# The halves of the mixed tensor packed: 344 columns apart in place of 384

## The chip, the cores and the metric

The kernel runs on one core of a Trainium2 chip. A core has a matrix engine (TensorE, PE in the profile, with its weight loads listed apart as PEld), a vector engine (DVE), a scalar engine (ACT), GpSimd (POOL), and queues that start DMA transfers (SP's and ACT's here). They run their own instruction streams and meet through semaphores. The metric is the device time of one execution in microseconds; the time of a kernel is the median of its runs.

## The reference

A layer-normalised input of 2048 tokens by 512 features goes through two branches, which are multiplied and added to the input. Branch A is attention over 32 heads with the last 512 keys of a cache. Branch B is a gated MLP that mixes tokens.

```python
def _B_ref(x, w_in, w_sp, b_sp, w_out):
    z = _gelu(jnp.einsum("bsd,df->bsf", x, w_in))
    z1 = z[..., :Fh]                                   # Fh = 688
    z2 = _layernorm(z[..., Fh:], axis=-1)
    g = jnp.einsum("ts,bsf->btf", w_sp, z2) + b_sp[None, :, None]
    return jnp.einsum("bsf,fd->bsd", z1 * g, w_out)

xn = _layernorm(x)
s = _A_ref(xn, ...)                                    # 32 heads, 512 keys each
g = _silu(_B_ref(xn, ...))
return x + s * g
```

What matters here is the product of w_sp (2048 x 2048) with z2 (2048 x 688), called the mixing below.

## The kernel before, in words

Everything is float32. Where a matmul needs more than one pass of the engine's reduced float32 type gives, each operand is held as two tiles, a rounded "hi" part and the rest, "lo". A product is then three matmuls (`mm3`, lines 61 to 63): hi by hi, hi by lo, lo by hi. The first operand of a matmul is the stationary one, which a weight load brings into the array; the second is the moving one, which is streamed from SBUF, one column per step.

The work has four stages, one behind the other, each in an order that is written out by hand.

- The input is normalised, transposed on TensorE and split into xh and xl; the first pieces of the product with w_in begin.
- The attention runs as one long software pipeline over 512 steps (32 heads by 16 blocks of 128 queries), with matmuls of 512 moving columns. The remaining z1 pieces (344 columns) are threaded through its first and last steps. z1 and the attention's sum s go to DRAM.
- The z2 stage (lines 447 to 493): for each of the 16 token tiles i, two products of 344 columns (`z_product`), gelu on ACT, statistics and normalisation on DVE, and `z_split`, which writes the hi part on ACT and the lo part on POOL (the last tile's on DVE) into the two z2 tiles.
- The mixing stage (from line 496). For each of the 16 output tiles i, `mix` runs over the 16 source tiles c and the two halves n, with `mm3` each: the stationary operands are w_sp's tile c (hi or lo), the moving ones z2's tile c, half n, 344 columns. That is 16 x 16 x 2 x 3 = 1536 matmuls. `gate` (DVE) adds the bias and multiplies with z1; the result goes through DVE's transpose and DRAM and comes back as stationary operand of `project`, 17 matmuls of 512 columns for each i, one tile behind the mixing. ACT and DVE split the w_sp pieces of the next tile meanwhile (`take`). The last tile has a shorter path of its own, with TensorE transposes and a projection in two halves of 256 columns.

The line that the change touches is the constant `ZW` (line 26), which is used in one place only, the shape of the two z2 tiles:

```python
zp = ctx.enter_context(tc.tile_pool(name="zp", bufs=1, side="right", reuse_waits="tile"))
z2 = (zp.tile([P, NT, 2, ZW], F32R, name="z2_h"), zp.tile([P, NT, 2, ZW], F32R, name="z2_l"))
zp.tile([P, 88], F32, name="gap")
```

The pool lies at the upper end of SBUF and ends there; the 88 columns of `gap` above the z2 tiles set where these end. A z2 tile is indexed by partition (128 tokens of a source tile), source tile (16), half (2) and column; `z_split` writes `t[:, i, :, :NB]` and `mix` reads `t[:, c, n, :NB]`, with NB = 344. With ZW = 384, 40 columns of each half are never written or read. A half takes 384 x 4 = 1536 bytes of each partition, a z2 tile 49,152. In the built program z2_h begins at byte 130,688 of each partition and z2_l at 179,840; both are 128 more than a multiple of 512, and since 1536 is three times 512, so is every operand in them. The other tiles that TensorE reads lie so too: each moving and each stationary operand of all 8828 matmuls begins 128 bytes past a multiple of 512.

Of the kernel before, what the change touches and what calls it, by code (L numbers as in the profile page):

```python
# [22 lines left out]
FH = 688  # L23
NB = FH // 2
NF = (FH + P - 1) // P
ZW = 384
EPS = 1e-5
NQ = S // 512
NBLK = H * NQ
# [9 lines left out]
def mixer_kernel(ctx: ExitStack, tc: tile.TileContext, x, wh, w_in, w_sp, b_sp, w_out, out):  # L39
# [382 lines left out]
# [3 lines that stand above are left out]
# [266 lines left out]
```

## Time and profile before

| | before |
|---|---|
| median of 3 runs | 1838.8 us (1837.55 to 1840.44) |
| the profiled execution | 1841.09 us, of it 1839.2 us from the first to the last instruction |
| granted TensorE clock, mean | 0.998 |
| TensorE busy | 1827.4 us, 99% of the span |
| weight loads busy | 1573.1 us, 86% |
| DVE, ACT, POOL busy | 74%, 55%, 48% |
| mixing stage | first ps_g matmul at 1537.0 us, last at 1826.3 us |

In the profile a group of instructions stands as "line engine operation out<-in shapes xcount | busy us, mean ns | idle time before, and what ended it". A matmul's duration is that of one passing through the array and overlaps with its neighbours; how fast they follow one another is seen from their starts in the timeline, whose lines begin with the start in us from the span's start and the duration in us. ps_g is the mixing's accumulator, z_h and z_l are z2's two parts, xh and xl in the mixing are w_sp's, ps_f is the projection's accumulator.

### The profile page before, as it was taken

How to read it: one execution, taken by the hardware profiler on the slowest of the kernel's cores; microseconds unless marked ns; L12 is line 12 of the kernel's file. 1: busy time of each engine (PE TensorE's matmuls, PEld its weight loads, DVE VectorE, ACT ScalarE, POOL GpSimd, SP SyncE). 2: the span in 40 equal slices, each digit the busy share in tenths (PEclk: the TensorE clock that was granted, in tenths of full speed). 3: DMA queues.
4: the chain of work that ended last, by engine and by line, in shares of the span. 5: the costliest groups of instructions: out<-in, count | busy, mean ns of one | idle time of the engine just before them, and what ended most of it. 6: DMA issues, size and time to landing. Idle time of an engine off the chain costs nothing.

```text
span 1839.2 us, 27426 instructions
## 1 busy us (share of the span) xinstructions
PE 1827.4 (99%) x8828; PEld 1573.1 (86%) x8828; DVE 1356.3 (74%) x2268; ACT 1019.4 (55%) x2188; POOL 873.6 (48%) x703
## 2 busy tenths in 40 slices
PE   8999999999999999999999999999999999999999
PEld 7888888888888888888888888888888999999998
DVE  7688888888888888888888888888888566333433
ACT  3566656666666665666666665665666445343422
POOL 3365555565565565555566555565566244000000
PEclk9999999999999999999999999999999999999999
DMA  5698888888888888888888888888888714554532
GB/s 190 179 234 216 217 219 224 215 218 218 221 214 217 216 219 217 216 214 217 219 224 217 218 216 226 215 218 217 218 215 225 222 65 153 174 184 140 182 120 91
DMA packets 404225, 369.69 MB, mean 201 GB/s; under 512 B 23056, under 2 KB 298768, under 8 KB 404080
## 3 DMA queue, kind: packets, MB, share of 16 engines
q1 hardware_dynamic: 399472, 362.30, 75.1%
q10 hardware_dynamic: 4608, 5.64, 0.9%
q8 instruction: 69, 1.13, 0.3%
q14 instruction: 76, 0.62, 0.1%
HBM read 213.70 MB, written 154.14 MB: 200 GB/s over the span
## 4 chain that ended last, share of the span: by engine, by line
PE 96%; DVE 1%; DMA 1%; ACT 1%; issue 0%; POOL 0%; ACTq 0%; SPq 0%; DVEq 0%; POOLq 0%
PE ps_a L61 14%; PE ps_a L62 14%; PE ps_a L63 14%; PE ps L63 13%; PE ps L61 13%; PE ps L62 13%; PE ps_g L61 4%; PE ps_g L62 4%; PE ps_g L63 4%; PE ps_f L63 1%; PE ps_f L62 1%; PE ps_f L61 1%; DMA z_dram<-z 0%; PE ps_f L621 0%; PE ps L166 0%
## 5 line engine op out<-in xcount | busy, mean ns | idle before, releaser
L57 POOL TENSOR_TENSOR pT_l<-pL,pT_h 128x512 fp32r<-128x512 f32 x507 | 658.6, 1299 | 572.1 <-ACT pT_h L256 526.2
L231 ACT ACTIVATE prob<-ps,nm 128x512 f32<-128x512 f32 x512 | 353.4, 690 | 533.6 <-DVE nm L229 531.5
L283 DVE SCALAR_TENSOR_TENSOR sacc<-ps,sums,sacc 128x512 f32<-128x512 f32 x496 | 370.7, 748 | 170.5 <-PE ps L63 170.4
L239 DVE STREAM_TRANSPOSE pB<-prob 128x512 f32<-128x512 f32 x512 | 359.4, 702 | 1.5 <-ACT pT_h L256 0.8
L229 DVE TENSOR_REDUCE nm<-ps 128x1 f32<-128x512 f32 x512 | 334.8, 654 | 3.6 <-PE ps L63 3.6
L256 ACT CAST pT_h<-pL 128x512 fp32r<-128x512 f32 x512 | 315.8, 617 | 7.6 <-ACT z L198 3.4
L61 PE MATMUL ps<-wh,qT_h 128*128 128x512 f32 x512 | 199.9, 390 | 0.9 <-DVE sacc L281 0.9
L63 PE MATMUL ps<-wh,oT_l 128*128 128x512 f32 x512 | 199.3, 389 | 0.3 <-DVE oT_l L57 0.3
L61 PE MATMUL ps_a<-xh,wh 128*128 128x512 f32 x512 | 199.4, 390 | 0.0
L62 PE MATMUL ps_a<-pT_l,wh 128*128 128x512 f32 x512 | 199.3, 389 | 0.0
L62 PE MATMUL ps_a<-xl,wh 128*128 128x512 f32 x512 | 199.3, 389 | 0.0
L62 PE MATMUL ps<-wl,qT_h 128*128 128x512 f32 x512 | 199.3, 389 | 0.0
L63 PE MATMUL ps_a<-xh,wl 128*128 128x512 f32 x512 | 199.2, 389 | 0.0
L63 PE MATMUL ps<-wh,qT_l 128*128 128x512 f32 x512 | 199.2, 389 | 0.0
L62 PE MATMUL ps<-wl,oT_h 128*128 128x512 f32 x512 | 199.2, 389 | 0.0
L61 PE MATMUL ps_a<-pT_h,wh 128*128 128x512 f32 x512 | 199.2, 389 | 0.0
L63 PE MATMUL ps_a<-pT_h,wl 128*128 128x512 f32 x512 | 199.2, 389 | 0.0
L61 PE MATMUL ps<-wh,oT_h 128*128 128x512 f32 x512 | 199.2, 389 | 0.0
L57 POOL TENSOR_TENSOR wl<-raw,wh 128x512 fp32r<-128x512 f32 (+1 forms) x132 | 169.6, 1286 | 37.0 <-ACT wh L120 37.0
L63 PE MATMUL ps_g<-z_h,xl 128*128 128x344 f32 x512 | 161.8, 316 | 0.0
L61 PE MATMUL ps_g<-z_h,xh 128*128 128x344 f32 x512 | 161.8, 316 | 0.0
L62 PE MATMUL ps_g<-z_l,xh 128*128 128x344 f32 x512 | 161.8, 316 | 0.0
(135 smaller groups left out, 2991.4 us busy)
## 6 DMA issues: line engine op xcount, KB each, us to landing
p_dram<-pB SPq DMA_DIRECT2D x512, 256.0 KB, 3.8
pL<-p_dram SPq DMA_DIRECT2D x512, 256.0 KB, 5.8
raw<-wh SPq DMA_DIRECT2D x128, 256.0 KB, 4.4
xh<-w_sp SPq DMA_DIRECT2D x32, 256.0 KB, 5.8
xl<-w_sp SPq DMA_DIRECT2D x28, 256.0 KB, 5.8
u_dram<-uB SPq DMA_DIRECT2D x15, 384.0 KB, 2.3
uL<-u_dram SPq DMA_DIRECT2D x60, 96.0 KB, 2.1
z_dram<-z ACTq DMA_DIRECT2D x32, 172.0 KB, 2.4
```

What stands on the lines that cost most here:

```text
L57: engine.tensor_tensor(lo, whole, hi.bitcast(F32), op=OP.subtract)
L61: nc.tensor.matmul(ps, lh, rh, start=first, stop=False)
L62: nc.tensor.matmul(ps, lh, rl, start=False, stop=False)
L63: nc.tensor.matmul(ps, ll, rh, start=False, stop=last)
L229: nc.vector.tensor_reduce(nm, ps, axis=AX.X, op=OP.max, negate=True)
L231: nc.scalar.activation(prob[t], ps, AF.Exp, bias=nm, accum_out=sums[b][:, j:j + 1])
L239: nc.vector.transpose(pB.rearrange("p (k q) -> p k q", q=Q), prob.pop(t))
L256: nc.scalar.copy(h, p)
L283: nc.vector.scalar_tensor_tensor(sacc[:, i, :], ps, rs, sacc[:, i, :], op0=OP.mult, op1=OP.add)
```

## The change

`ZW` becomes 344, so that the halves of a tile lie directly one behind the other.

```diff
--- before
+++ after
@@ -23,7 +23,7 @@
 FH = 688
 NB = FH // 2
 NF = (FH + P - 1) // P
-ZW = 384
+ZW = 344
 EPS = 1e-5
 NQ = S // 512
 NBLK = H * NQ
```

A half is now 1376 bytes of each partition and a z2 tile 44,032. In the built program z2_h begins at byte 140,928 and z2_l at 184,960, again 128 past a multiple of 512, but the 32 operands of each z2 tile follow one another in steps of 1376 bytes, which is 2 x 512 + 352. Modulo 512 they begin at the sixteen multiples of 32, two operands at each. The writes of `z_split` become one run of 688 columns in place of two runs of 344. The stationary operands, all other tiles, the instructions and their order on each engine stay; the first copy into z2_h waits for one DMA queue fewer, since z2_h no longer covers some of the buffers that lay there before.

## The prediction

> **What bounds the kernel now.** I read the page first (busy shares, the chain that ended last, the costliest groups), then the windows of the mixing stage, the waits of TensorE, and last the timeline of single matmuls, because the change touches nothing but the places of one stage's operands.
>
> ```profile
> span 1839.2 us, 27426 instructions
> PE 1827.4 (99%) x8828; PEld 1573.1 (86%) x8828; DVE 1356.3 (74%) x2268; ACT 1019.4 (55%) x2188; POOL 873.6 (48%) x703
> PE 96%; DVE 1%; DMA 1%; ACT 1%; issue 0%; POOL 0%; ACTq 0%; SPq 0%; DVEq 0%; POOLq 0%
> L63 PE MATMUL ps_g<-z_h,xl 128*128 128x344 f32 x512 | 161.8, 316 | 0.0
> L61 PE MATMUL ps_g<-z_h,xh 128*128 128x344 f32 x512 | 161.8, 316 | 0.0
> L62 PE MATMUL ps_g<-z_l,xh 128*128 128x344 f32 x512 | 161.8, 316 | 0.0
> ```
>
> TensorE is busy 99% of the span and carries 96% of the chain. The mixing is the three ps_g groups: 3 x 512 = 1536 matmuls of 344 columns, none of which found the engine idle. Windows inside the stage, and TensorE's waits from 1460 us to the end, say the same:
>
> ```profile
> 1555.00:1575.00 20.00, 20.00 (x124) 19.34 (x123) 8.29 (x15) 6.62 (x9) 0.00 (x0) 1.00 0.66 208
> 1700.00:1750.00 50.00, 50.00 (x310) 48.60 (x310) 19.24 (x32) 20.31 (x27) 0.00 (x0) 1.00 0.53 173
> PE ps L63 <- DVE oT_l L57: 0.3, 1, 0.3
> ```
>
> The columns are the stretch, its length, then busy time and count for PE, weight loads, DVE, ACT, POOL, the granted clock, DMA share and GB/s. TensorE is busy all of the time at granted clock 1.00, the vector engines well under half, and the one wait listed is of 0.3 us and lies in the attention's tail. So from 1537 to 1826 us the time is the number of matmuls times their spacing, and only the spacing can move it. The 316 ns of a row is a pipelined duration; the spacing is read from starts in the timeline:
>
> ```profile
> 100.44 0.39 PE L61 MATMUL ps<-wh,oT_h 128*128 128x512 f32 x1
> ...
> 113.81 0.39 PE L63 MATMUL ps_a<-pT_h,wl 128*128 128x512 f32 x1
> ...
> 1607.42 0.32 PE L61 MATMUL ps_g<-z_h,xh 128*128 128x344 f32 x1
> ...
> 1615.70 0.32 PE L61 MATMUL ps_g<-z_h,xh 128*128 128x344 f32 x1
> ...
> 1833.06 0.28 PE L61 MATMUL ps_g<-wo_h,xh 128*128 128x256 f32 x1
> ...
> 1834.98 0.28 PE L621 MATMUL ps_g<-xl,xh 128*128 128x256 f32 x1
> ```
>
> Between the pairs lie 59, 54 and 16 steps: 13.37/59 = 226.6 ns for 512 columns, 8.28/54 = 153.3 ns for 344, 1.92/16 = 120.0 ns for 256. From 256 to 512 columns a column costs (226.6 - 120.0)/256 = 0.417 ns, so 344 columns alone are 143.3 ns; a mixing matmul carries 10.0 ns beside its columns, the others 13.3 (120.0 - 106.7). All three spacings are whole multiples of 6.67 ns (34, 23 and 18): the stream seems to start on a fixed grid. I call this the settled spacing. The trace also shows an unsettled one:
>
> ```profile
> 45.72 0.32 PE L61 MATMUL ps<-pT_h,xh 128*128 128x344 f32 x1
> 45.88 0.31 PE L62 MATMUL ps<-pT_l,xh 128*128 128x344 f32 x1
> 46.03 0.32 PE L63 MATMUL ps<-pT_h,xl 128*128 128x344 f32 x1
> ...
> 47.61 0.39 PE L61 MATMUL ps_a<-xh,wh 128*128 128x512 f32 x1
> ...
> 1473.84 0.50 PE L63 MATMUL ps<-wh,oT_l 128*128 128x512 f32 x1 [0.31 <-DVE oT_l L57]
> 1474.18 0.39 PE L61 MATMUL ps<-wh,oT_h 128*128 128x512 f32 x1
> ...
> 1476.26 0.32 PE L61 MATMUL ps_a<-wh,xh 128*128 128x344 f32 x1
> ```
>
> In the first stage twelve 344-column matmuls in a row took 1.89 us, 157.5 ns each; after the stall at 1473 us nine 512-column ones took 2.08 us, 231.1 ns each. The engine waited for nothing in between and the clock was 1.00. The same shapes therefore run 4.2 and 4.5 ns above the settled spacing when something in their timing does not line up.
>
> **The change part by part.** *Addresses.* In the built program each of the 8828 moving operands and each stationary operand begins 128 bytes past a multiple of 512. With ZW = 344 a half is 1376 bytes, which is 2 x 512 + 352, so the 32 (tile, half) operands of each z2 tile spread over sixteen places, two at each, 32 bytes apart; only two keep 128. The place changes after every three matmuls: the two z_h and one z_l reads of a triple agree. The instructions, their order on each engine and their shapes stay. No row of before shows an operand at another place, so the price has to be bounded.
>
> From below: without any of the 10.0 ns a matmul could gain 10.0, or 1.5 of the 6.67 ns grid steps; one whole step is 6.67. From above: the nearest rows are the unsettled ones (+4.2 ns); further off, the whole overhead could be paid twice or the weight load could be slowed until it no longer hides.
>
> ```profile
> L62 PEld LDWEIGHTS ps_g<-z_l,xh 128*128 128x128 f32 x512 | 96.1, 188 | 0.5
> ```
>
> That row gives a weight load 188 ns of latency, more than the spacing, yet 256-column matmuls with weights of the same size come every 120.0 ns, so loads have 33 ns of room in the mixing (153.3 - 120.0). I therefore take +13.3 ns, two grid steps, as the upper end and -6.67 as the lower one.
>
> I choose +4.2, the nearest row in kind: the same shape and weights, in another alignment in time. The reason to take it rather than zero: an engine whose starts keep a grid as long as each stream begins at the same place is given a different place after every third matmul, so it has to settle anew 512 times. Term one: 1536 x 4.2 ns = 6.4 us.
>
> *Projections.* Between the mixings lie 15 projections of 17 matmuls of 512 columns, all at the old place. If the mixing leaves TensorE unsettled, they begin so; the rows after the stall show nine matmuls that stay so, about half of 17. 255 x 4.5 ns = 1.1 us, half of it 0.6.
>
> *The split copies.* ACT's, POOL's and DVE's writes of z2 become one contiguous run of 688 columns in place of two of 344.
>
> ```profile
> L475 ACT CAST z_h<-z x16: 759/766/769, 1489.7 to 1542.3; 128x688 fp32r<-128x688 f32 x16
> L57 POOL TENSOR_TENSOR z_l<-z,z_h x15: 1662/1672/1687, 1490.6 to 1542.5; 128x688 fp32r<-128x688 f32 x15
> 1543.10 1.79 DVE L57 TENSOR_TENSOR z_l<-z,z_h 128x688 fp32r<-128x688 f32 x1 [1.01 <-ACT z_h L475]
> ...
> 1550.78 0.32 PE L61 MATMUL ps_g<-z_h,xh 128*128 128x344 f32 x1
> ```
>
> I cost them at nothing. They hide under the z products. The last one ends at 1543.10 + 1.79 = 1544.9 us and the first matmul that reads tile 15 starts at 1550.78: 5.9 us of cover. If each of POOL's 15 grew by 0.3 us, 4.5 us would still fit; beyond the cover the excess would stall the first mixing.
>
> *Placement.* z2_h now begins 10240 bytes higher and clears the buffers of the z1 output and a part of sacc, so the first z_h copy waits for fewer DMA queues. The copies' waits in this trace end on DVE's normalisation, and TensorE waits for none of them: nothing gained.
>
> Sum: 6.4 + 0.6 = 7.0 us. The profiled execution took 1841.1 us, its span and 1.9 around it, so it would become 1848.1; it stands 2.3 us above the median of 1838.8, so against the median I get 1845.8, about 1846.
>
> **The rivals.** *No effect.* The matmul's reads are blind to where an operand begins, and the spacing stays 153.3. For it: nothing in the trace varies the place, and the unsettled rows show that time alone, with all places equal, can unsettle the engine. Against it: it leaves the grid unexplained. Time 1838.8. The Trainium skill ("TensorE: Matmul & The Clock Gate", Part 2, step 1) says that the array has independent read ports for the moving operand and the weights, and that loading the next weights takes no bandwidth from the running matmul; by that rule this rival holds. The trace agrees that loads hide, but the 10.0 ns beside the columns is not the 2.5 ns that its section "Back-to-back issue gap" gives, so I do not let it decide.
>
> *Faster.* Weights and moving data now all begin at the same place modulo 512, so the two streams may meet in the same part of the memory; this could be what the 10.0 ns are. In the changed kernel 30 of 32 operands begin elsewhere. If that frees one grid step in each, 1440 x 6.67 ns = 9.6 us go: 1829.2. If only the first matmul of a triple gains, 512 x 6.67 = 3.4 us: 1835.4. It decides once the first matmul of a triple starts less than 153 ns before the second. Against it: equal places also held for 256 and 512 columns and the overhead there is 13.3, not growing with the columns, which fits a fixed cost per matmul better than a meeting of streams.
>
> *Only the change of place costs.* One grid step at the first matmul of a triple: 512 x 6.67 ns = 3.4 us, 1842.2. For it: unsettled at 45 us, settled at 100 us, so the engine finds its spacing again in between.
>
> *A true collision.* The new places cost two grid steps in each matmul that left the old one: 1440 x 13.3 ns = 19.2 us, 1858.0. No row speaks for it but the room above.
>
> **How the numbers follow.** Unsettled mixing 0.50; no effect 0.14; faster 0.16; change of place alone 0.10; collision 0.10. A measurement of this kernel tells about 0.2%, 3.7 us, from no change. Unsettled and collision are slower beyond that, and a fifth of the change-of-place case is: 0.62. The rest of it and no effect make 0.22. Faster 0.16. The range 1834 to 1860 leaves out most of the faster case and the worst of collisions, some 0.17; the likeliest case alone has 1842 to 1850 (4.2 ns in only half of the matmuls, or 7 in all).
>
> **What would show it.** Right: starts in the mixing 155 to 160 ns apart and uneven, the ps_g stage about 6 us longer, projections between 226.6 and 231 ns, and all before 1537 us as it was. Wrong: 153.3 throughout (no effect), a regular 146.7 (faster), 160 in one of three (change of place), or idle time of TensorE at tile 15 of the first mixing (the copies). A spacing that differs by place, with some of the sixteen at 153.3 and others far above, would mean that the place itself has a price, which my terms do not hold.

## The result and the profile after

The changed kernel takes 1844.6 us (median of 9 runs, 1842.5 to 1846.0) against 1839.3 us before (9 runs, 1837.2 to 1840.4). The ratio is 1.003 with a 95% interval of 1.002 to 1.004: slower by 0.3%, some 5 us, where 1846 was forecast.

The page of the changed kernel, then two windows in the same columns as before, then TensorE's waits from 1460 us on:

```profile
span 1844.2 us, 27425 instructions
PE 1831.8 (99%) x8828; PEld 1576.4 (85%) x8828; DVE 1356.0 (74%) x2268; ACT 1019.8 (55%) x2188; POOL 873.4 (47%) x703
PE 96%; DVE 1%; DMA 1%; ACT 1%; issue 0%; POOL 0%; ACTq 0%; SPq 0%; DVEq 0%; POOLq 0%
L61 PE MATMUL ps_g<-z_h,xh 128*128 128x344 f32 x512 | 163.5, 319 | 0.0
L62 PE MATMUL ps_g<-z_l,xh 128*128 128x344 f32 x512 | 163.1, 319 | 0.0
L63 PE MATMUL ps_g<-z_h,xl 128*128 128x344 f32 x512 | 163.0, 318 | 0.0
```

```profile
1555.00:1575.00 20.00, 20.00 (x121) 19.31 (x121) 7.93 (x14) 6.43 (x9) 0.00 (x0) 1.00 0.63 206
1700.00:1750.00 50.00, 50.00 (x300) 48.12 (x299) 20.15 (x33) 20.31 (x27) 0.00 (x0) 1.00 0.53 168
```

```profile
PE ps L63 <- DVE oT_l L57: 0.3, 1, 0.3
```

TensorE is as busy as before at the same clock, waits for as little, and gets through fewer matmuls in the same stretch (121 where there were 124, 300 where there were 310). Nothing waits more; each matmul of one stage takes longer. The starts show how. The view is the timeline of TensorE: eight triples, then the same point eight triples on, and the projection behind them.

```profile
1609.70 0.32 PE L61 MATMUL ps_g<-z_h,xh 128*128 128x344 f32 x1
1609.85 0.32 PE L62 MATMUL ps_g<-z_l,xh 128*128 128x344 f32 x1
1610.01 0.32 PE L63 MATMUL ps_g<-z_h,xl 128*128 128x344 f32 x1
1610.17 0.32 PE L61 MATMUL ps_g<-z_h,xh 128*128 128x344 f32 x1
...
1613.46 0.32 PE L61 MATMUL ps_g<-z_h,xh 128*128 128x344 f32 x1
...
1617.22 0.32 PE L61 MATMUL ps_g<-z_h,xh 128*128 128x344 f32 x1
...
1623.33 0.40 PE L61 MATMUL ps_f<-wo_h,xh 128*128 128x512 f32 x1
...
1627.21 0.32 PE L61 MATMUL ps_g<-z_h,xh 128*128 128x344 f32 x1
```

Twenty-four matmuls take 3.76 us, 156.7 ns each, and then another 3.76. The single steps lie between 151 and 163 ns, but they repeat from one group of eight operands to the next, and 3.76 us is 564 steps of 6.67 ns: the engine is on its grid again only after eight operands. Over the 1536 mixing matmuls the steps add up to 240.56 us against 235.52 before, so the mean went from 153.3 to 156.6 ns and the stage grew by 5.04 us. The 17 projection matmuls from 1623.33 to 1627.21 took 3.88 us, 228.2 each; the 238 of them between 1540 and 1822 us together are 0.37 us longer. Up to the mixing there is no loss: its first matmul starts 0.46 us earlier than before, at 1536.5 us. The sum, 5.04 + 0.37 - 0.46, is the 5.0 us between the spans.

### The profile page after: what moved, and what is told of

Its sections match the earlier page's. It is cut to its first block, busy times and chain, and to the rows that moved or that the text cites. A ratio compares the mean times of both kernels' runs of the same rounds, so it can differ in the third digit from the quotient of the medians.

```text
span 1844.2 us, 27425 instructions
## 1 busy us (share of the span) xinstructions
PE 1831.8 (99%) x8828; PEld 1576.4 (85%) x8828; DVE 1356.0 (74%) x2268; ACT 1019.8 (55%) x2188; POOL 873.4 (47%) x703
## 4 chain that ended last, share of the span: by engine, by line
PE 96%; DVE 1%; DMA 1%; ACT 1%; issue 0%; POOL 0%; ACTq 0%; SPq 0%; DVEq 0%; POOLq 0%
PE ps_a L63 14%; PE ps_a L61 14%; PE ps_a L62 14%; PE ps L63 13%; PE ps L61 12%; PE ps L62 12%; PE ps_g L61 4%; PE ps_g L63 4%; PE ps_g L62 4%; PE ps_f L61 1%; PE ps_f L62 1%; PE ps_f L63 1%; DMA z_dram<-z 0%; PE ps_f L621 0%; PE ps L166 0%
## 5 line engine op out<-in xcount | busy, mean ns | idle before, releaser
L61 PE MATMUL ps<-wh,qT_h 128*128 128x512 f32 x512 | 199.9, 390 | 1.0 <-DVE sacc L281 1.0
L63 PE MATMUL ps<-wh,oT_l 128*128 128x512 f32 x512 | 199.3, 389 | 0.3 <-DVE oT_l L57 0.3
L61 PE MATMUL ps_a<-xh,wh 128*128 128x512 f32 x512 | 199.5, 390 | 0.0
L62 PE MATMUL ps_a<-pT_l,wh 128*128 128x512 f32 x512 | 199.3, 389 | 0.0
L62 PE MATMUL ps_a<-xl,wh 128*128 128x512 f32 x512 | 199.3, 389 | 0.0
L63 PE MATMUL ps_a<-xh,wl 128*128 128x512 f32 x512 | 199.3, 389 | 0.0
L62 PE MATMUL ps<-wl,qT_h 128*128 128x512 f32 x512 | 199.2, 389 | 0.0
L63 PE MATMUL ps<-wh,qT_l 128*128 128x512 f32 x512 | 199.2, 389 | 0.0
L61 PE MATMUL ps_a<-pT_h,wh 128*128 128x512 f32 x512 | 199.2, 389 | 0.0
L61 PE MATMUL ps<-wh,oT_h 128*128 128x512 f32 x512 | 199.2, 389 | 0.0
L62 PE MATMUL ps<-wl,oT_h 128*128 128x512 f32 x512 | 199.2, 389 | 0.0
L63 PE MATMUL ps_a<-pT_h,wl 128*128 128x512 f32 x512 | 199.2, 389 | 0.0
L61 PE MATMUL ps_g<-z_h,xh 128*128 128x344 f32 x512 | 163.5, 319 | 0.0
L62 PE MATMUL ps_g<-z_l,xh 128*128 128x344 f32 x512 | 163.1, 319 | 0.0
L63 PE MATMUL ps_g<-z_h,xl 128*128 128x344 f32 x512 | 163.0, 318 | 0.0
```

Source lines behind the costliest of these rows:

```text
L61: nc.tensor.matmul(ps, lh, rh, start=first, stop=False)
L62: nc.tensor.matmul(ps, lh, rl, start=False, stop=False)
L63: nc.tensor.matmul(ps, ll, rh, start=False, stop=last)
```

## The experiments

The theory that I went in with was that of the prediction: what costs is the *change of place* after every three matmuls. The rival was that the *place* itself has a price. The first four kernels tell them apart: two keep one place for all of z2 but not the old one, two keep the change of place but use rounder steps. In all of them the summary to look at is the row of the 512 L61 matmuls: minimum, median and maximum duration, and first and last start, whose difference is the length of the stage. Before it reads:

```profile
L61 PE MATMUL ps_g<-z_h,xh x512: 316/316/316, 1537.0 to 1826.0; 128*128 128x344 f32 x171
```

289.0 us, with a single duration. The changed kernel:

```profile
L61 PE MATMUL ps_g<-z_h,xh x512: 314/320/323, 1536.5 to 1830.9; 128*128 128x344 f32 x171
```

294.4 us, with durations that differ.

### All of z2 at another place

```diff
-    zp.tile([P, 88], F32, name="gap")
+    zp.tile([P, 120], F32, name="gap")     # e1: all at 0; e2 has 80 columns: all at 160
```

> ZW stays 384 and the gap grows from 88 to 120 columns, so that all 32 operands of each z2 tile begin at 0 modulo 512, and the stationary ones stay at 128. If the change of place from triple to triple is what costs (theory), there is no change here: spacing in the mixing 153.3 ns, time as before within 2 us. If a place other than 128, or one that differs from the stationary operand's, has a price of its own (rival), the spacing is even but above 153.3 ns, or uneven, 155 to 158 ns, and the time 3 to 8 us above before.

> ZW stays 384 and the gap shrinks to 80 columns: all z2 operands begin at 160 modulo 512, half a 64-byte block beside the old place. Theory (only a change of place costs): 153.3 ns and the time of before. Rival (a place has a price): above 153.3 ns; after the changed kernel's triples at 160, about 157 ns, which would be 5 to 6 us above before. If only the distance to a multiple of 64 bytes matters, this one is slow and the one at 0 is not.

e1 took 1847.4 us against 1840.3, ratio 1.0036 (1.0024 to 1.0047); e2 1845.9, ratio 1.0027 (1.0018 to 1.0037). The rows of e1 and then e2:

```profile
L61 PE MATMUL ps_g<-z_h,xh x512: 314/318/324, 1535.5 to 1831.1; 128*128 128x344 f32 x171
```

```profile
L61 PE MATMUL ps_g<-z_h,xh x512: 318/318/323, 1535.9 to 1830.8; 128*128 128x344 f32 x171
```

295.6 and 294.9 us: as slow as the changed kernel or slower, though the place never changes. From the starts, e1's spacing is 157.2 ns in a pattern that repeats after seven matmuls (1.10 us, 165 grid steps); e2's is an even 156.7. My theory falls here. The place does have a price, and a distance from the nearest multiple of 64 bytes does not explain it, since 0 is slow.

### The change of place with rounder steps

```diff
-ZW = 384
+ZW = 352     # e3: places 128, 0, 384, 256; e4 has 368: the eight multiples of 64
```

> ZW = 352: the place still changes after every three matmuls, but over four places only, all multiples of 128 bytes (128, 0, 384, 256). Theory (each change of place costs): as slow as the changed kernel, spacing 156 to 158 ns, 4 to 6 us above before. Rival (what costs is a place that is not a multiple of 64 or 128 bytes): 153.3 ns and the time of before.

> ZW = 368: a change of place after every three matmuls over eight places, all multiples of 64 bytes. Theory (each change of place costs): 156 to 158 ns, 4 to 6 us above before. Rival (blocks of 64 bytes): 153.3 ns, time of before. Rival (blocks of 128 bytes, if ZW = 352 is fast): between 154 and 157 ns, half of its places being off.

e3: 1845.6 us, ratio 1.0026 (1.0016 to 1.0035); e4: 1846.5, ratio 1.0027 (1.0017 to 1.0036). Both have a mean spacing of 156.6 ns. That is also the number the fallen theory expected, so this pair alone could not have refuted it. What it refutes are the blocks of 64 or 128 bytes, by which e3 would have kept 153.3 ns. e3 holds a hint, though: from the starts, its triples at place 128 take 153.1 ns a matmul, those at 0, 384 and 256 take 158.5, 156.7 and 158.0.

### Is it 128 itself, or the distance from the stationary operand?

All stationary operands lie at 128 too, so the two readings are the same until the stationary ones move. A pad ahead of all other tiles moves everything except z2 to 0; with the larger gap z2 goes along.

```diff
+    const.tile([P, 96], F32, name="pad")   # e5 and e6
     ident = const.tile([P, P], F32, name="ident")
...
-    zp.tile([P, 88], F32, name="gap")      # e6 only
+    zp.tile([P, 120], F32, name="gap")
```

> A pad of 96 columns (384 bytes) ahead of all other tiles moves every tile but z2 from 128 to 0 modulo 512; ZW = 384 and z2 stays at 128. Theory now (what counts is the distance of the moving operand from the stationary one modulo 512): attention and projections keep 226.7 ns, the mixing's spacing is 156 to 158 ns as it was with z2 at 0 and the rest at 128, time 5 to 7 us above before. Rival (the place 128 itself is the good one): the mixing stays at or near 153.3 ns and the attention's 512-column spacing goes to about 231 ns, which over its 6144 matmuls is 25 us and more above before.

> The same pad, and the gap at 120 columns, so that z2 lies at 0 modulo 512 too: all moving and all stationary operands at 0. Theory (distance): 153.3 ns in the mixing, 226.7 ns elsewhere, the time of before. Rival (the place 128 itself): attention at about 231 ns, mixing at about 157 ns, 30 us above before.

e5, with z2 where it was before the change, took 1845.6 us against 1840.4, ratio 1.0031 (1.0019 to 1.0044); e6, with not one operand of TensorE at its old place, 1839.7, ratio 0.9998 (0.9989 to 1.0008). The rows of e5 and e6:

```profile
L61 PE MATMUL ps_g<-z_h,xh x512: 314/318/324, 1535.8 to 1831.4; 128*128 128x344 f32 x171
```

```profile
L61 PE MATMUL ps_g<-z_h,xh x512: 316/316/316, 1535.3 to 1824.3; 128*128 128x344 f32 x171
```

295.6 and 289.0 us. In both, the attention's 512-column matmuls, whose two operands moved together, follow one another at 226.7 ns as before. So neither of the two places, 0 and 128, is good or bad; what counts is how far the moving operand's start lies from the stationary operand's. This is the test that settles the main question.

### Which distances

Three probes measure the spacing at one constant place after the other. The mixing of output tile i reads source tile i alone, in all of its 96 matmuls, so the work has the same size; ZW sets how far the place moves with each i.

```diff
-ZW = 384
+ZW = 388     # e7, e8: 32 bytes per tile; e12 has 385: 8 bytes per tile
...
-                        tuple(t[:, c, n, :NB] for t in z2))
+                        tuple(t[:, i, 0, :NB] for t in z2))     # e8: half 1, 16 bytes further
```

(e12 also has pads that bring both z2 tiles to the same place.) Each probe has one execution, of which only the steps between the starts are used.

> A measurement of the place alone. ZW = 388, and the mixing of output tile i reads source tile i, half 0, in all of its 96 matmuls in place of the sixteen tiles and two halves (so the output is not the reference's). The tile's place is 32 bytes further for each i, so each i gives the spacing of 96 matmuls at one constant place. Theory (distance from the stationary operand at 128): 153.3 ns at 128, 157.2 at 0, 156.7 at 160, and values between 155 and 159 at the others. Rival (only even distances such as 256 matter): 153.3 at 384 as well. If a place gives 146.7 ns it would be a way to beat both kernels.

> As the probe before, with half 1 of tile i in place of half 0, which lies 16 bytes further: the sixteen places are the odd multiples of 16 bytes (the output is not the reference's here either). Theory (distance): none at 153.3, all between 155 and 159 ns. Rival (blocks of 64 bytes decide): all alike or as the nearest multiple of 32; a place at 146.7 would again be a way to beat both.

> The probe of the place with finer steps: ZW = 385, the two z2 tiles at one place, and the mixing of output tile i reads tile i, half 0, in all of its 96 matmuls (the output is not the reference's). The places go from 128 to 248 in steps of 8 bytes. Theory (distance modulo 256): 153.3 at 128; 156.0 at 144, 156.7 at 160, 156.3 at 176, 156.0 at 192, 159.9 at 240 as in the probes before. Open is 136, 8 bytes off: between 153.3 and 156 if a meeting of two streams needs the same 16 bytes, 155 to 159 if the exact place decides.

In e7's timeline, the first and the last start of the 96 matmuls at place 288 and at place 384:

```profile
1625.55 0.32 PE L61 MATMUL ps_g<-z_h,xh 128*128 128x344 f32 x1
...
1640.75 0.32 PE L63 MATMUL ps_g<-z_h,xl 128*128 128x344 f32 x1
...
1682.83 0.32 PE L61 MATMUL ps_g<-z_h,xh 128*128 128x344 f32 x1
...
1697.40 0.32 PE L63 MATMUL ps_g<-z_h,xl 128*128 128x344 f32 x1
```

15.20 us / 95 = 160.0 ns and 14.57 / 95 = 153.4 ns. So 256 bytes off is settled too, which was the rival's expectation and not mine. All places of the three probes, read in this way, with the distance from the stationary operand taken modulo 256 (where two places have the same distance so taken, they agree within 0.1 ns):

| distance, bytes | 0 | 8 | 16 | 24 | 32 | 40 | 48 | 56 | 64 | 72 | 80 | 88 |
|---|---|---|---|---|---|---|---|---|---|---|---|---|
| ns per matmul | 153.3 | 159.9 | 156.0 | 159.0 | 156.7 | 160.0 | 156.2 | 157.8 | 156.0 | 157.4 | 157.8 | 160.0 |

| distance, bytes | 96 | 104 | 112 | 120 | 128 | 144 | 160 | 176 | 192 | 208 | 224 | 240 |
|---|---|---|---|---|---|---|---|---|---|---|---|---|
| ns per matmul | 157.5 | 160.1 | 159.9 | 160.0 | 157.2 | 159.9 | 160.0 | 157.7 | 159.9 | 158.7 | 155.6 | 156.0 |

Of the distances measured, only 0 and 256 keep 153.3; each other one costs 2.3 to 6.7 ns, the most being one step of 6.67. Eight bytes are enough for nearly all of that, which is above both ranges expected for them. None is below 153.3, so there is no place among these that would beat the kernel before. The kernels above that keep one distance fit the table: e1 and e5, both 128 bytes off in opposite directions, have 157.2 ns, and e2, 32 off, has 156.7. The table is for one distance held over 96 matmuls and does not add up where distances change: e3's triples at place 384 are 256 off and take 156.7 ns, not 153.3, and in the changed kernel the means by place run from 154.9 to 159.3 ns, with none at 153.3. The period of 256 also explains why the changed kernel's steps repeat after eight operands and not after sixteen: 8 x 1376 = 11,008 is 43 x 256.

### A change of place that keeps the distance

```diff
+    zp.tile([P, 64], F32, name="mid")      # between z2_h and z2_l
...
-    zp.tile([P, 88], F32, name="gap")
+    zp.tile([P, 24], F32, name="gap")
```

> z2_l alone moves to 384 modulo 512 (pad of 64 columns, gap 24), 256 bytes off, so the place changes between each two matmuls of a triple. Theory (distance modulo 256, and a change of place costs nothing): 153.3 ns, the time of before within 2 us. Rival (the change of place has a part in the cost, the step of the prediction): more than 153.3 ns, 2 to 6 us above before.

e11 took 1838.9 us against 1841.0, ratio 0.9991 (0.9981 to 1.0001), which cannot be told from no difference.

```profile
L61 PE MATMUL ps_g<-z_h,xh x512: 316/316/316, 1532.9 to 1821.9; 128*128 128x344 f32 x171
```

289.0 us, 153.3 ns, although the place changes between each two matmuls of a triple. The change costs nothing. (That the stage begins 4 us earlier in this execution is no part of the comparison: in the kernels above its start lies anywhere from 1534.5 us, in e4, to 1537.8, in e3, with the same work ahead of it.)

### Which of the two weights: the matmul's own, or those being loaded for the next?

While a matmul streams, the weights of the next one are loaded: in the mixing before, that load starts 3 or 4 ns behind the matmul's start and takes 188 ns. A meeting of these two would make the distance to the *next* weights count. e9 moves z2_l alone by 128 bytes; e10 moves w_sp's low part xl by 128 bytes too, which makes each stream agree with the load beside it (zl with xl, zh with xh) and two of three disagree with their own weights.

```diff
+    zp.tile([P, 32], F32, name="mid")      # e9 and e10, between z2_h and z2_l; gap 56
...
+            if g == 0:                     # e10 only, between the xh and the xl buffers;
+                xp.tile([P, 32], F32, name="pad_a", bufs=1)     # pad_b of 96 behind xl
```

> z2_l alone moves to 256 modulo 512 (a pad of 32 columns between the z2 tiles, gap 56), 128 bytes off; z2_h and all stationary operands stay at 128. So one matmul in three of the mixing has a distance of 128 bytes. Both readings of the distance theory (to the weights being loaded for the next matmul, or to the matmul's own weights) expect the mixing unsettled: 154 to 158 ns in the mean, at least one of the three kinds off 153.3. If the price were paid by the third alone, 153.3 + 3.9/3 = 154.6 ns.

> As the run before, and w_sp's low part xl moves to 256 modulo 512 too (pads of 32 columns ahead of the xl buffers and 96 behind them; xl of the attention and of the projection moves with it, so the whole time is not compared). In a triple, zl streams while xl is being loaded for the next matmul, and zh streams while xh is being loaded. If the distance that counts is that to the weights being loaded (theory: the load meets the running stream), all distances are 0 again: 153.3 ns in the mixing. If it is the distance to the matmul's own weights (rival), two of three matmuls are 128 off, zl against xh and zh against xl: 154 to 158 ns.

Each has one execution, 1850.3 us for e9 and 1853.1 for e10; as xl is used in other stages too, the comparison goes by the mixing alone. The rows of e9 and e10:

```profile
L61 PE MATMUL ps_g<-z_h,xh x512: 316/317/321, 1538.7 to 1835.2; 128*128 128x344 f32 x171
```

```profile
L61 PE MATMUL ps_g<-z_h,xh x512: 315/319/321, 1541.3 to 1838.0; 128*128 128x344 f32 x171
```

296.5 and 296.7 us, mean spacing 157.8 and 157.7 ns. One matmul in three at a wrong distance already costs more than sixteen places do, because its two neighbours leave 153.3 too: in e9 the steps from z_l's matmul are 160.8 ns, those from the other two 155.9 and 156.8. And e10 is not settled, which is what the rival, the matmul's own weights, expected: agreement with the weights being loaded is not enough.

e10 has more places to look, since xl is a moving operand in the attention (the projection of q) and a stationary one in the z2 stage and in the output projection. A moving operand that is off among settled neighbours, in its attention:

```profile
600.67 0.39 PE L61 MATMUL ps_a<-xh,wh 128*128 128x512 f32 x1
600.90 0.40 PE L62 MATMUL ps_a<-xl,wh 128*128 128x512 f32 x1
601.14 0.39 PE L63 MATMUL ps_a<-xh,wl 128*128 128x512 f32 x1
601.36 0.39 PE L61 MATMUL ps_a<-pT_h,wh 128*128 128x512 f32 x1
```

The rows are rounded to 10 ns; over the 411 such triples from 300 to 1440 us the step from the xl matmul is 234 or 235 ns, the one behind it 225 or 226, and all others 226 or 227. One wrong distance (here both to its own weights and to those being loaded) costs about one grid step, 6.67 ns, and the engine is settled again at once. In the output projection xl is the weights of every L63; the rows with PEld are the weight loads:

```profile
1611.81 0.39 PE L61 MATMUL ps_f<-wo_h,xh 128*128 128x512 f32 x1
1611.81 0.19 PEld L62 LDWEIGHTS ps_f<-wo_l,xh 128*128 128x128 f32 x1
1612.03 0.40 PE L62 MATMUL ps_f<-wo_l,xh 128*128 128x512 f32 x1
1612.04 0.19 PEld L63 LDWEIGHTS ps_f<-wo_h,xl 128*128 128x128 f32 x1
1612.27 0.40 PE L63 MATMUL ps_f<-wo_h,xl 128*128 128x512 f32 x1
1612.27 0.19 PEld L61 LDWEIGHTS ps_f<-wo_h,xh 128*128 128x128 f32 x1
1612.50 0.39 PE L61 MATMUL ps_f<-wo_h,xh 128*128 128x512 f32 x1
```

In the 14 projections between the mixings, behind the first six matmuls of each, the step from L61 (neither weights nor load off) is 226 or 227 ns, from L62 (xl is being loaded) 232 or 233, from L63 (xl is its own weights) 234 or 235: two grid steps to a triple. The z2 stage has the same mismatch with 344 columns, and does otherwise. Over its 132 triples the step from L62 (xl is being loaded) is 158.0 ns in the mean, from L63 (xl is its own weights) 153.3, and from L61 155.3, where before all were 153.3: one grid step to a triple, and none of it at L63. So in both stages the step beside a load that is off is longer. Whether a matmul's own weights count for themselves stays open: e10's mixing, where every load is in place and the own weights of two matmuls in three are not, speaks for it, and its z2 stage against it. What in the memory or in the array the 256 bytes are stays open too.

## Why the prediction was right or wrong

The time was right, the reason given for it was not.

- *Only the spacing of the mixing can move the time*: right. TensorE's waits, clock and busy share are the same, and the steps between mixing matmuls, 5.04 us, are the whole of the 5.0 us between the spans but for two small terms that nearly cancel.
- *Term one, 1536 x 4.2 = 6.4 us*: 1536 x 3.28 = 5.04 us. The size came near, 4.2 forecast and 3.28 measured, and that is luck in part. The unsettled rows of the first stage, the changed kernel and all kernels with a wrong distance lie between 155.6 and 160.1 ns; but in the first stage every operand begins at the same place, so what unsettled them is not what the change did.
- *The reason for taking it* is the step that failed: that an engine given "a different place after every third matmul" has "to settle anew 512 times". The place never changes in e1, e2 and e5, which are as slow; it changes twice in each triple in e11, which is as fast as before. What the change broke is the equal start, modulo 256, of moving and stationary operands: with 1376 bytes to a half, 28 of 32 operands of a z2 tile lie at another distance.
- *Projections, 0.6 us*: 0.37 us measured over the 14 that lie between the mixings (the prediction counts 15, but the last stands behind them). They do begin unsettled, and settle after five of their 17 matmuls, not half.
- *Split copies at nothing*: right.

```profile
L475 ACT CAST z_h<-z x16: 757/760/771, 1489.2 to 1541.8; 128x688 fp32r<-128x688 f32 x16
L57 POOL TENSOR_TENSOR z_l<-z,z_h x15: 1664/1670/1684, 1490.1 to 1542.0; 128x688 fp32r<-128x688 f32 x15
```

ACT's and POOL's medians are 760 and 1670 ns, where they were 766 and 1672. The fewer queues that the first copy waits for show in nothing either.

- *The rival "no effect"*: refuted. With the same instructions in the same order, the relative place of the two operands alone moves the spacing from 153.3 to as much as 160.1 ns, by 4%. The Trainium skill ("TensorE: Matmul & The Clock Gate", Part 2, step 1) says that loading the next weights takes no read bandwidth from the running matmul. The traces do not fit a reading of that rule by which places are free; that a load takes bandwidth is not shown either.
- *The rival "faster"* named the right quantity, the equal places of weights and moving data, and the wrong sign: equal places are the fast case.
- *"Only the change of place costs"*: refuted by e11. *"A true collision"*, +13.3 ns: no mean spacing measured in the mixing is more than one grid step, 6.7 ns, above the settled one.
- *The sign of a price of the place*, some places at 153.3 and others far above: the changed kernel's own trace does not show it (154.9 to 159.3 ns by place), the probes do, for the distance.

## What to carry to other kernels

Where a stage is a train of matmuls with nothing else on its path, look at the starts in the timeline and not at the durations: the spacing tells apart two kernels whose busy shares are the same. With operands of the reduced float32 type, as here, keep the start of the moving operand at the same place modulo 256 bytes as the start of the weights (a pad or a gap in a pool is enough; other types were not measured), and check it again after any edit of a tile's row length, since a shape that saves 40 columns of memory moved every later operand. The price of not doing so is small, 2.3 to 6.7 ns per matmul in the mean here, but every matmul of the stage pays it.

## What the runs showed of the hardware that was not expected

- The settled spacing of back-to-back matmuls is a whole number of steps of 6.67 ns: 120.0 (256 columns), 153.3 (344) and 226.7 (512) are 18, 23 and 34 of them. The unsettled patterns leave this grid and come back to it, after 24 matmuls in the changed kernel (564 steps), after 7 in e1 (165 steps) and after 2 in e2, whose even 156.7 ns are 23.5 steps.
- The spacing in the mixing depends on the distance between the starts of moving and stationary operand modulo 256 bytes and not on either place, as far as the places were moved: 153.3 ns at 0 and 256, 155.6 to 160.1 at 23 other distances; 8 bytes off cost 6.6 ns.
- Equal starts are not all that it takes. Before the change every matmul has them, and yet the first stage ran 344 columns at 157.5 ns at 45 us. No run here shows what unsettles these.
- A single wrong distance among right ones cost about one step in e10's attention (234 or 235 ns, then 225 or 226), and the matmuls behind were back at 226.7.
